# A fused linear-attention, mixture and routed-expert kernel: the mixture's last expert in plain products, routing on fifteen tiles instead of twelve

## The chip, the cores and the metric

The kernel runs on one core of a Trainium2 chip. The metric is the time in microseconds (us) of one execution on the device, as the median of several; lower is better. PE (TensorE) does the matmuls, and PEld is its weight load; DVE (VectorE), ACT (ScalarE) and POOL (GpSimd) do elementwise work; SP and POOL issue the DMAs spoken of here.

## The reference

Three stages over 2304 tokens of width 512 (8 heads of 64):

```
kv  = einsum('bhsd,bhde->..', k, v);  out = q @ kv;  x = out / rms(out) * g_norm      # per head
p   = domain_probs / (domain_probs.sum(-1) + 1e-9)                                    # 4 experts, all of them for every token
x   = sum over e of p[:, e] * (relu(x @ w1[e]) @ w2[e])                                # w1[e] 512x1024, w2[e] 1024x512
...
idx = argmax(normalised x @ normalised expert_emb.T / tau)                             # 8 experts, one for each token
out[idx == e] = gate_w * (relu(x[idx == e] @ w1b[e]) @ w2b[e])
```

The second mixture's router needs a token's finished sum over all four experts of the first one.

## The kernel before, in words

**Precision.** Each product is done as three matmuls of operands split in a high and a low part (hi*hi, hi*lo, lo*hi): ACT casts the high part (L61), DVE subtracts it to get the low part (L62 for weights, L768 `hl` for hidden values).

**Attention** of a tile of 128 tokens is a chain: transpose of q (`qt_unit`, `psq` L142), product with kv (`x_unit`, `psx` L159, copied by ACT to `xs` L173), RMS-norm on DVE (`x_norm`, from L175), transpose back (`xt_unit`, `psxt` L204). `att(tiles)` lists these for one or two tiles. They are scattered over the phases of the first mixture.

**First mixture.** The 18 tiles form 6 units of 3 tiles, and the units 3 pairs p = 0, 1, 2. A phase (p, e, fh) does one pair, one expert e, one half fh of its 1024 hidden columns: first L1 (x times w1, L793), then L2 (hidden times w2, L888), whose result DVE scales and adds to the tile's sum, `acc` (L897); the last such sum of tiles 12 to 17 goes to `fin`. From the second expert on, L1 is done by Strassen's scheme (7 products for 8) on sums of blocks of x (`x_fills`: b11, t1 and so on, made on POOL and DVE) and of w1 (`w1_sums`). Expert 0 of pair 0 is done in four plain phases, one unit and one half each (`plain_unit`, L781). `run_steps(steps, todo, pace)` writes a phase out: after each step come the pieces of `todo` that are due by a hand-written time (in model units; a Strassen phase is about 30 long, a plain one 16.6), and `background(n)` takes n pieces of a queue `bg` with n from `pace`: logits and routing. The order in which the code is written is the order on each engine; an engine waits in place.

**Routing.** When a tile's sum is done it is written to DRAM, `x1d`. Its router logits come in one of two ways: `logits_v` reloads it as `row` and does eight dot products on DVE (L314); `logits_t` transposes it on PE (`pslt` L324) and multiplies by the embeddings (`psl` L329). `route_a` runs once the first TA = 12 tiles have logits: it counts tokens per expert (`psr` L393), gives each its place, builds one-hot matrices `po` on DVE (L338), and inverts the placement by matmuls (`psi` L454) to indices `ix`. From these, `gather` fetches the token rows of NA = 4 full jobs (`xg` L694). `route_b` does the same for all the other tokens after tile 17.

**Second mixture.** 25 slots of 128 tokens (22 filled for this data), each: gather, transpose (`pstx` L1136), w1 (`m1`, `psm` L1146), w2 (L1168), scaled output `y` on ACT (L1172), scatter. A slot's weights, 8 DMAs of 512 KB, are loaded only where the expert changes.

Of the kernel before, what the change touches and what calls it, by code (L numbers as in the profile page):

```python
# [20 lines left out]
def attn_moe_moe_kernel(ctx: ExitStack, tc: tile.TileContext, q, k, v, g_norm, dprobs, w1, w2, emb, tau, w1b, w2b, out):  # L21
    nc = tc.nc
# [995 lines left out]
    sm = st_p.tile([128, NT, 1], F32, name="sm", tag="sm")
    nc.vector.tensor_reduce(out=sm, in_=dp, axis=AX.X, op=ALU.add)
    nc.vector.tensor_scalar_add(sm, sm, 1e-9)  # L1020
    nc.vector.reciprocal(sm, sm)
    nc.vector.tensor_tensor(out=dp, in0=dp, in1=sm.to_broadcast([128, NT, E1]), op=ALU.mult)
# [27 lines left out]
    order = [(0, 0), (0, 1), (1, 1), (1, 0)]  # L1050
    for at_ph, (un, fh) in enumerate(order):
        steps = [(P1T / 4, lambda f=f: plain_unit(un, f)) for f in range(4)]
        steps += l2_steps(0, fh, [un], None, first_half, (P2T - P1T) / 6)
        todo = []
        if at_ph != 2:
            todo += spread([lambda n=n: fill_w2(0, 2 * fh + n) for n in range(2)], 0, P1T)
        if at_ph == 0:
            w1_blocks(0, 1)
            todo += [(-1, f) for f in plain_direct(1)]
            todo += [(2.5, lambda: nc.gpsimd.tensor_tensor(  # L1060
                out=xr[:, 0].rearrange("p c n -> p (c n)"), in0=xf_t[0][:, 0:2 * XW].bitcast(F32), in1=xf_t[1][:, 0:2 * XW].bitcast(F32), op=ALU.add))]
            todo += [(1.5 + 2 * p, lambda p=p: kv_unit(1, p)) for p in range(NP)]
            todo += [(7.9, lambda: w1_blocks(0, 2)), (16.0, lambda: w1_blocks(0, 3))]
            todo += spread(plain_direct(2), 8.5, 12) + spread(plain_direct(3), 16.1, 16.6)
            todo += spread(att(range(TS, TS + 1)), 9, P2T)
        if at_ph == 1:
            todo += spread(att(range(TS + 1, 2 * TS)), 0, 13)
            todo += [(13.2, lambda: x_split(6, xblock(0, 1))), (14.5, xs_f["b22"])]
        if at_ph == 2:
            todo += [(7.9, lambda: w1_blocks(0, 0)), (12.0, lambda: w1_blocks(0, 1))]  # L1070
            todo += spread(plain_direct(0), 8.5, 12) + spread(plain_direct(1), 12.1, 16)
            todo += spread([xs_f[n] for n in ("t1", "t3", "x1", "x3", "t2", "x2", "t4")], 0, P2T)
        if at_ph == 3:
            todo += [(7.5, lambda: w1_sums(1, 0)), (8.5, xs_f["x4"])]
            todo += spread(w1_fills(1, 0), 9, 12) + [(12.1, lambda: w1_sums(1, 1))] + spread(w1_fills(1, 1), 12.2, P2T)
        run_steps(steps, todo, [0] * len(steps))

    ahead = {
        (0, 1, 0): spread(att([6]), 16, S2T),
# [10 lines left out]
        (1, 3, 0): spread(att([17]), 0, S2T),  # L1090
        (2, 0, 0): [(20.0, end_attention)],
    }
    for at_ph, ph in enumerate(strassen):
# [13 lines left out]
        last = at_ph + 1 == len(strassen)  # L1107
        if last:
            todo += [(6.5, lambda: late.update(slots=True)), (14.7, lambda: late.update(weights=True))]
        pace = [4 if last else 0 if i % 2 else 1 for i in range(len(steps))]  # L1110
        if last:
            pace[-1] = 0
        run_steps(steps, todo, pace)
# [157 lines left out]
```

## Time and profile before

| | us |
|---|---|
| median of 3 runs (lowest, highest) | 1193.28 (1192.33, 1194.89) |
| the profiled execution | 1194.21 |
| its span, first to last instruction | 1192.4 |
| first mixture, first plain phase to last L2 matmul | 26.6 to 872.1 |
| output y of slot 1, 2 and the last used slot | 932.4, 944.7, 1174.7 |

The span is 1.8 us less than the execution's own time, and that 0.9 more than the median. Times inside the span are from its first instruction. In the timeline, a bracket at the end of a row gives the idle time of the engine before it and what it waited for.

### The profile page before, as it was taken

Reading aid. Unit: us, or ns where it says so; the run is one execution under the profiler, and the core shown is the slowest. Engines: PE = TensorE matmul, PEld = TensorE weight load, DVE = VectorE, ACT = ScalarE, POOL = GpSimd, SP = SyncE. Lnnn points to the kernel's source line nnn. Section 1 sums busy time; section 2 is a strip of 40 time slices with the busy share of each in tenths; the row PEclk is TensorE's granted clock in tenths of the full one; section 3 lists DMA queues with packets and bytes.
Section 4 is the critical chain, followed back from the end, with each engine's and each line's share of the span. In section 5 each row is a group of like instructions: output and inputs, shape, how many; then the busy total and the mean of one; then the engine's idle time right before and its main releaser. Section 6 shows DMA issues by size and latency. Waiting matters only on the chain. (4 is left out here: it accounts for less than half of the span.)

```text
span 1192.4 us, 17373 instructions
## 1 busy us (share of the span) xinstructions
PE 1116.8 (94%) x5902; PEld 974.9 (82%) x5902; DVE 754.9 (63%) x1300; ACT 566.4 (47%) x1010; POOL 292.1 (24%) x344
## 2 busy tenths in 40 slices
PE   8999999998999999999999999999784999999993
PEld 7789888997888989889889888789563888888882
DVE  3557564664986787666978878775358662465350
ACT  3435446543555444444554444344354664566450
POOL 3102333220433233212433333122010211121120
PEclk9999999999999999999999999999897999999997
DMA  9413254221334223211332222123433863665460
GB/s 257 140 48 108 79 159 133 80 71 54 106 106 133 89 72 88 71 55 52 105 108 80 75 70 77 53 71 89 139 121 138 288 216 103 210 233 212 148 218 12
DMA packets 87971, 139.18 MB, mean 117 GB/s; under 512 B 17269, under 2 KB 51061, under 8 KB 87744
## 3 DMA queue, kind: packets, MB, share of 16 engines
q1 hardware_dynamic: 80432, 113.56, 29.9%
q0 software_dynamic: 7440, 24.41, 6.1%
q8 instruction: 49, 0.80, 0.3%
q14 instruction: 50, 0.41, 0.1%
HBM read 183.03 MB, written 10.49 MB: 162 GB/s over the span
## 5 line engine op out<-in xcount | busy, mean ns | idle before, releaser
L888 PE MATMUL bank<-w2h,hh 128*128 128x512 f32 x576 | 230.8, 401 | 6.1 <-DVE acc L897 4.6
L888 PE MATMUL bank<-w2h,hl 128*128 128x512 f32 x576 | 228.0, 396 | 1.9 <-DVE hl L768 1.9
L888 PE MATMUL bank<-w2l,hh 128*128 128x512 f32 x576 | 227.3, 395 | 0.0
L62 DVE TENSOR_TENSOR w2l<-raw,w2h 128x1024 fp32r<-128x1024 f32 x98 | 117.8, 1222 | 108.5 <-ACT w2h L61 107.8
L793 PE MATMUL bank<-xth,w1h 128*128 128x384 f32 x616 | 160.8, 342 | 6.3 <-DVE acc L897 3.8
L793 PE MATMUL bank<-xtl,w1h 128*128 128x384 f32 x616 | 157.4, 336 | 0.0
L793 PE MATMUL bank<-xth,w1l 128*128 128x384 f32 x616 | 157.2, 336 | 0.0
L888 PEld LDWEIGHTS bank<-w2h,hh 128*128 128x128 f32 x576 | 109.5, 190 | 29.7 <-DVE acc L897 4.8
L888 PEld LDWEIGHTS bank<-w2h,hl 128*128 128x128 f32 x576 | 109.4, 190 | 28.7 <-DVE hl L768 5.1
L888 PEld LDWEIGHTS bank<-w2l,hh 128*128 128x128 f32 x576 | 109.6, 190 | 21.2
L897 DVE SCALAR_TENSOR_TENSOR acc<-bank,dp,acc 128x512 f32<-128x512 f32 x120 | 89.6, 746 | 52.9 <-PE bank L888 52.5
L793 PEld LDWEIGHTS bank<-xth,w1h 128*128 128x128 f32 x616 | 109.8, 189 | 11.4 <-ACT w1h L61 4.6
L793 PEld LDWEIGHTS bank<-xtl,w1h 128*128 128x128 f32 x616 | 112.0, 189 | 0.0
L793 PEld LDWEIGHTS bank<-xth,w1l 128*128 128x128 f32 x616 | 111.7, 188 | 0.0
L61 ACT CAST w2h<-raw 128x1024 fp32r<-128x1024 f32 x98 | 101.3, 1056 | 3.7 <-DMA raw<-in_moe_w_dram 2.5
L62 DVE TENSOR_TENSOR w1l<-raw,w1h 128x512 fp32r<-128x512 f32 (+2 forms) x131 | 87.7, 690 | 24.2 <-ACT w1h L61 23.2
L804 POOL TENSOR_TENSOR sv<-sv,s 128x384 f32<-128x384 f32 x44 | 47.5, 1079 | 225.9 <-ACT sv L800 215.9
L800 ACT COPY s<-bank 128x384 f32<-128x384 f32 x88 | 42.1, 478 | 102.9 <-PE bank L793 102.9
L606 POOL TENSOR_TENSOR wsum<-raw 128x256 f32<-128x256 f32 x44 | 37.9, 862 | 189.7 <-issue 141.2
L61 ACT CAST w1h<-wsum 128x1024 fp32r<-128x1024 f32 x44 | 46.1, 1048 | 72.4 <-POOL wsum L609 72.4
L314 DVE CUSTOM_DVE_ANT_0 scr<-row,en_b 128x512 bf16<-128x512 f32 x96 | 78.0, 813 | 0.1
L1173 POOL DMA_INDIRECT out_dram<-y,ix x22 | 22.4, 1019 | 217.3 <-ACTq L734 95.1
(246 smaller groups left out, 1973.3 us busy)
## 6 DMA issues: line engine op xcount, KB each, us to landing
raw<-in_moe_w_dram SPq DMA_DIRECT2D x300, 512.0 KB
raw<-in_k_dram SPq DMA_DIRECT2D x12, 256.0 KB
raw<-in_v_dram SPq DMA_DIRECT2D x12, 256.0 KB
qraw<-in_q_dram POOLq DMA_DIRECT2D x12, 256.0 KB, 4.0
x1d<-acc POOLq DMA_DIRECT2D x12, 256.0 KB, 2.5
row<-x1d POOLq DMA_DIRECT2D x12, 256.0 KB, 4.3
en_b<-in_moe_expert_emb_dram POOLq DMA_DIRECT2D x1, 2048.0 KB
x1d<-fin POOLq DMA_DIRECT2D x6, 256.0 KB, 2.3
```

What stands on the lines that cost most here:

```text
L61: nc.scalar.copy(hi, raw)
L62: (eng or nc.vector).tensor_tensor(out=lo, in0=raw, in1=hi.bitcast(F32), op=ALU.subtract)
L314: nc.vector.tensor_tensor_reduce(out=scr, in0=x, in1=en_b[:, e], scale=1.0, scalar=0.0, op0=ALU.mult, op1=ALU.add, accum_out=lg[:, t, e:e + 1]
L606: gt(out=sm[:, 0], in0=a21, in1=a22, op=ALU.add)
L793: nc.tensor.matmul(out=ps, lhsT=wform(wo, b, w)[:, c], rhs=xform(xo, x)[:, c], start=start and n == 0, stop=(n == 5), skip_group_check=True)
L800: nc.scalar.copy(t, src)
L804: (eng or nc.vector).tensor_tensor(out=out, in0=a, in1=b, op=ALU.add)
L888: nc.tensor.matmul(out=ps, lhsT=h_t[o][f][u][:, ns], rhs=w[j][:, a], start=(k == 0 and m == 0), stop=(k == 3 and m == 2))
L897: nc.vector.scalar_tensor_tensor(out=fin, in0=ps, scalar=dp[:, t, e:e + 1], in1=ac, op0=ALU.mult, op1=ALU.add)
L1173: nc.gpsimd.indirect_dma_start(out=out[:, :], out_offset=bass.IndirectOffsetOnAxis(ap=ix[:, col(s):col(s) + 1], axis=0), in_=y, in_offset= ...
```

## The change

- NA, NB become 8 and 17, TA 15 tiles: `route_a` takes tiles 0 to 14 and makes 8 full jobs.
- The last expert of the last pair is done in four plain phases: unit 4 with halves 0 and 1, then unit 5 with halves 1 and 0. Tiles 12 to 14 are so finished two phases before the first mixture's end. The first of w1's and w2's halves is loaded a second time (2 MB more). One block of x that the Strassen scheme has overwritten is rebuilt in the last Strassen phase (`x_back`: three sums and a split on DVE).
- `logits_v` is used for tiles 0 to 13, `logits_t` from 14 on.
- In `att` of two tiles, the first tile's `xt_unit` comes ahead of the second's `x_unit`.
- In the first phase, the normalising of the mixture's weights `dp` moves from ahead of the phase into it, and a sum `xr`, one 128x1536 addition on POOL, becomes four 128x384 on DVE.
- Of the block sums between pairs, two (t3, x3) come earlier and three (b21, t4, x4) go into the next pair's first phase.

```
-    NA, NB, R = 4, 21, 5
-    TA = 4 * TS
+    NA, NB, R = 8, 17, 5
+    TA = 5 * TS
...
+        return [
+            step(xform(0, 2).bitcast(F32), xform(1, 2), ALU.add),
+            step(t, xform(0, 5), ALU.subtract),
+            step(t, xform(1, 5), ALU.subtract),
+            lambda: x_split(6, t),
+        ]
...
+    stream += raws(E1 - 1, 0) + raws(E1 - 1, 1) + raws(E1 - 1, 0)
...
-        last = e == E1 - 1 and fh == 1
+        last = e == E1 - 1 and fh == ((t // TS) % 2 == 0 or t < N // 128 - 2 * TS)
...
-            bg.append((logits_v if t < TA else logits_t)(t, ac))
+            bg.append((logits_v if t < TA - 1 else logits_t)(t, ac))
...
             u.append(lambda t=t: qt_unit(t))
+            if prev is not None:
+                u.append(lambda t=prev: xt_unit(t))
             u.append(lambda t=t: x_unit(t))
             u.append(lambda t=t: x_norm(t))
-            if prev is not None:
-                u.append(lambda t=prev: xt_unit(t))
             prev = t
...
+    def plain_phase(un, e, fh, todo, pace):
+        steps = [(P1T / 4, lambda f=f: plain_unit(un % 2, f)) for f in range(4)]
+        steps += l2_steps(e, fh, [un], None, first_half, (P2T - P1T) / 6)
+        run_steps(steps, todo, pace)
...
-            todo += [(2.5, lambda: nc.gpsimd.tensor_tensor(
...
+    todo += [(1.5 + 2 * p, lambda p=p: kv_unit(1, p)) for p in range(NP)] + [(6.0, norm_probs)]
+    todo += [(10.0 + c, lambda c=c: nc.vector.tensor_tensor(
+        out=xr[:, 0, c], in0=xform(0, 0, 2)[:, c].bitcast(F32), in1=xform(1, 0, 2)[:, c].bitcast(F32), op=ALU.add)) for c in range(NC)]
...
+            todo += [(14.8 + 2 * i, f) for i, f in enumerate(x_back())]
...
-            todo += [(4.0, xs_f["b11"]), (4.2, xs_f["t1"])]
-            todo += spread([xs_f[n] for n in ("x1", "t2", "x2", "b22", "t3", "x3", "b21", "t4", "x4")], 14.8, 26)
...
+            todo += [(4.0, xs_f["b11"]), (5.5, xs_f["t1"]), (7.0, xs_f["t3"]), (10.0, xs_f["x3"])]
+            todo += spread([xs_f[n] for n in ("x1", "t2", "x2", "b22")], 14.8, 26)
+            carried = [(0.5, xs_f["b21"]), (3.0, xs_f["t4"]), (6.0, xs_f["x4"])]
...
+    e, u = E1 - 1, UNITS - 2
+    plain_phase(u, e, 0, w2_fills(e, 0) + w1_plain_fills(e, 1), [1] * 99)
+    plain_phase(u, e, 1, w2_fills(e, 1), [1] * 99)
+    plain_phase(u + 1, e, 1, w1_plain_fills(e, 0), [2] * 99)
+    todo = w2_fills(e, 0) + [(7.5, lambda: late.update(slots=True)), (8.3, lambda: late.update(weights=True))]
+    plain_phase(u + 1, e, 0, todo, [4] * 9 + [0])
```

Code behind the diff's first new lines stands 12 to 29 lines further down than before: L897 is L914 in the changed kernel, L888 L905, L768 L785, L1136 L1165.

Three places in the order of the instructions. First DVE, in the first phase, between the last split of the first tiles and the second half of w1's splits (`sm`, `dp`: the mixture's weights; `w1l`, `w2l`, `hl`: low parts). Before:

```order
L212 SCALAR_TENSOR_TENSOR xtl<-psxt,g_74,xth 128x4x128 x3
L1019 TENSOR_REDUCE sm<-dp 128x18
L1020 TENSOR_SCALAR sm<-sm 128x18
L1021 RECIPROCAL sm<-sm 128x18
L1022 TENSOR_TENSOR dp<-dp,sm 128x72
L768 SCALAR_TENSOR_TENSOR hl_133<-bank,hh_125 128x384
L62 TENSOR_TENSOR w1l<-raw,w1h 128x512
L62 TENSOR_TENSOR w1l<-raw,w1h 128x256 x2
L62 TENSOR_TENSOR w2l_87<-raw,w2h_85 128x1024
```

After:

```order
L785 SCALAR_TENSOR_TENSOR hl_133<-bank,hh_125 128x384
L62 TENSOR_TENSOR w1l<-raw,w1h 128x512
L62 TENSOR_TENSOR w1l<-raw,w1h 128x256 x2
L62 TENSOR_TENSOR w2l_87<-raw,w2h_85 128x1024
L785 SCALAR_TENSOR_TENSOR hl_135<-bank,hh_127 128x384
L785 SCALAR_TENSOR_TENSOR hl_137<-bank,hh_129 128x384
L1037 TENSOR_REDUCE sm<-dp 128x18
L1038 TENSOR_SCALAR sm<-sm 128x18
L1039 RECIPROCAL sm<-sm 128x18
L1040 TENSOR_TENSOR dp<-dp,sm 128x72
```

The four instructions on `sm` and `dp` now stand behind the first low parts of w1 and w2. Second PE, in L2 of phase (0,3,0), where tiles 10 and 11 get their attention. Before:

```order
L142 MATMUL psq<-ident,qraw 128x128 x4
...
L888 MATMUL bank<-w2h_85,hl_135 128x512
L159 MATMUL psx<-kvbd_142,qT 128x128 x4
...
L888 MATMUL bank<-w2h_86,hl_138 128x512
L204 MATMUL psxt<-ident,xs 128x128 x4
```

After:

```order
L142 MATMUL psq<-ident,qraw 128x128 x4
...
L905 MATMUL bank<-w2h_85,hl_135 128x512
L204 MATMUL psxt<-ident,xs 128x128 x4
...
L905 MATMUL bank<-w2h_85,hl_133 128x512
...
L159 MATMUL psx<-kvbd_142,qT 128x128 x4
```

The transpose of tile 10 (`psxt`), which reads the only buffer `xs`, stands ahead of tile 11's product instead of 5 groups of L2 behind it. Third DVE, at the first mixture's end (`fin`: the sum of tile 17; `gs`, `ix`: the inverted placement). After:

```order
L334 TENSOR_TENSOR rhs<-so,ids 128x15x8 x2
L334 TENSOR_TENSOR rhs<-so,gp 128x15x8 x3
L914 SCALAR_TENSOR_TENSOR fin<-bank,dp,acc_124 128x512
L338 TENSOR_SCALAR po<-lane_b,pos 128x128 x15
L461 COPY gs<-psi 128x8
L462 SCALAR_TENSOR_TENSOR ix<-gs,psi 128x8
L463 COPY gs<-psi 128x8
L334 TENSOR_TENSOR gs<-gs,psi 128x8 x2
L62 TENSOR_TENSOR xtl<-raw,xth 128x1024 x4
L334 TENSOR_TENSOR xgl<-pstx,xgh 128x512
```

On PE the 15 `psi` of `route_a` stand behind the last L2 matmul, right ahead of slot 0's `pstx`. Before, `route_a`'s `po` came in phase (2,3,0), with its 12 `psi` among that phase's L1 matmuls, and what stood behind the last L2 matmul was slot 0 itself; `route_b`'s 18 `po` stood behind the first slot.

## Rows read from the trace of the kernel before

**Rows 1.** The page: busy time, share of the span, instructions of the engines.
```profile
PE 1116.8 (94%) x5902; PEld 974.9 (82%) x5902; DVE 754.9 (63%) x1300; ACT 566.4 (47%) x1010; POOL 292.1 (24%) x344
```

**Rows 2.** Stretches: length, busy PE, PEld, DVE, ACT, POOL (instructions), PEclk, DMA share, GB/s.
```profile
26.60:43.14 16.54, 14.17 (x129) 12.12 (x129) 10.36 (x14) 6.33 (x15) 4.92 (x4) 0.90 0.61 155
53.22:78.33 25.11, 22.92 (x127) 20.10 (x126) 13.21 (x27) 11.88 (x21) 1.78 (x2) 0.93 0.30 85
78.33:94.86 16.53, 16.53 (x86) 15.08 (x85) 10.11 (x15) 7.45 (x14) 0.00 (x0) 1.00 0.08 27
247.59:288.70 41.11, 36.52 (x189) 32.66 (x188) 23.15 (x40) 16.92 (x32) 10.30 (x13) 0.96 0.22 65
321.82:339.41 17.59, 17.59 (x96) 17.55 (x97) 15.86 (x29) 9.45 (x18) 9.47 (x11) 0.90 0.55 165
624.62:655.57 30.95, 30.95 (x158) 28.10 (x156) 25.64 (x48) 14.28 (x27) 10.09 (x11) 1.00 0.25 77
751.45:786.95 35.50, 32.54 (x162) 28.31 (x160) 27.92 (x70) 14.40 (x27) 7.70 (x10) 1.00 0.19 60
940.00:953.00 13.00, 13.00 (x67) 10.90 (x66) 12.03 (x14) 11.72 (x16) 2.55 (x2) 1.00 0.99 351
```

**Rows 3.** What PE's matmuls waited for, 100 to 787 us: total, times, longest.
```profile
PE bank L793 <- DVE acc L897: 3.8, 2, 1.9
```

**Rows 4.** Timeline of PE, places with idle time: start, length, idle before.
```profile
36.23 0.69 PE L781 MATMUL bank<-xth,w1l 128*128 128x384 f32 x1 [2.37 <-DVE w1l L62]
...
72.14 0.41 PE L204 MATMUL psxt<-ident,xs 128*128 128x128 f32 x2 [2.19 <-DVE xs L181]
...
281.05 0.50 PE L888 MATMUL bank<-w2h,hh 128*128 128x512 f32 x1 [4.59 <-DVE acc L897]
...
873.53 0.48 PE L1146 MATMUL psm<-xth,xgh 128*128 128x512 f32 x1
...
920.36 3.04 PE L454 MATMUL psi<-rhs,po 128*128 128x105 bf16 x18 [15.45 <-DVE po L338]
```

**Rows 5.** Timeline of DVE and POOL in the first phase.
```profile
31.30 3.81 DVE L1022 TENSOR_TENSOR dp<-dp,sm 128x72 f32<-128x72 f32 x1
...
31.53 3.48 POOL L1060 TENSOR_TENSOR xr<-xth,xtl 128x1536 f32<-128x1536 f32 x1
...
35.50 1.34 DVE L62 TENSOR_TENSOR w1l<-raw,w1h 128x512 fp32r<-128x512 f32 x3
```

**Rows 6.** Timeline of DVE in the second half of phase (0,3,0).
```profile
277.12 0.69 DVE L175 TENSOR_REDUCE ms<-xs 128x8 f32<-128x512 f32 x1 [8.24 <-ACT xs L173]
```

**Rows 7.** The tile row: its instructions on DVE; its reloads.
```profile
L314 DVE CUSTOM_DVE_ANT_0 scr<-row,en_b x96: 669/684/1522, 320.3 to 739.4; 128x512 bf16<-128x512 f32 x96
...
DMA to landing us min/median/max: 3.0/3.4/5.7
```

**Rows 8.** Groups by line and form on DVE, 787 to 932 us.
```profile
L62 DVE TENSOR_TENSOR w2l<-raw,w2h 128x1024 fp32r<-128x1024 f32 x12 | 14.4, 1218 | 9.7 <-ACT w2h L61 9.7
L897 DVE SCALAR_TENSOR_TENSOR fin<-bank,dp,acc 128x512 f32<-128x512 f32 x6 | 4.5, 749 | 8.1 <-PE bank L888 8.1
L768 DVE SCALAR_TENSOR_TENSOR hl<-bank,hh 128x384 fp32r<-128x384 f32 x4 | 2.2, 554 | 1.3 <-ACT hh L765 1.3
```

**Rows 9.** Timeline of DVE at the end of the second routing.
```profile
911.75 0.23 DVE L338 TENSOR_SCALAR job<-job,ho 128x21 f32<-128x21 f32 x1
...
917.06 0.18 DVE L334 TENSOR_TENSOR gp<-ga,gp 128x18 bf16<-128x18 f32 x1
...
920.06 3.01 DVE L338 TENSOR_SCALAR po<-lane_b,pos 128x128 bf16<-128x128 bf16 x18
```

**Rows 10.** The gathers of token rows: issue to landing.
```profile
DMA to landing us min/median/max: 3.3/4.2/7.9
```

**Rows 11.** Timeline of ACT: the outputs y of slots 1 and 2.
```profile
932.41 0.70 ACT L1172 ACTIVATE y<-psy,gs 128x512 f32<-128x512 f32 x1
...
944.68 0.70 ACT L1172 ACTIVATE y<-psy,gs 128x512 f32<-128x512 f32 x1
```

More of the change, by code (lines that the diff above doesn't have):

```diff
@@ L648, in x_fills, with x_back, step @@
         }
+    def x_back():
+        t = sum_p.tile([128, 4, 2, 128], F32, name="wsum", tag="wsum").rearrange("p a b c -> p (a b c)")[:, 0:XW]
+        t = t.rearrange("p (c t) -> p c t", t=SUB)
+        def step(a, b, op):
+            return lambda: nc.vector.tensor_tensor(out=t, in0=a, in1=b.bitcast(F32), op=op)
+        return [
[4 more added lines that the diff above has]
+        ]
     def raws(e, fh):
@@ L653, in attn_moe_moe_kernel @@
     stream += [("kv", 0, n) for n in range(NP)] + raws(0, 0) + raws(0, 1) + raws(0, 0)
-    strassen = [(p, e, fh) for p in range(UNITS // 2) for e in range(E1) for fh in range(2) if p or e]
+    END = (UNITS // 2 - 1, E1 - 1)
+    strassen = [(p, e, fh) for p in range(UNITS // 2) for e in range(E1) for fh in range(2) if (p or e) and (p, e) != END]
     KV_AT = {(0, 2, 0): 2, (1, 0, 1): 3}
@@ L895, in l2_unit @@
         else:
-            fin = late["tmp"].tile([128, D], F32, name="fin", tag="fin", bufs=2) if last and t >= TA else ac
+            fin = late["tmp"].tile([128, D], F32, name="fin", tag="fin", bufs=3) if last and t >= TA else ac
             nc.vector.scalar_tensor_tensor(out=fin, in0=ps, scalar=dp[:, t, e:e + 1], in1=ac, op0=ALU.mult, op1=ALU.add)
@@ L1017, in attn_moe_moe_kernel, with norm_probs @@
     issue()
[L1018 to L1022, printed above, removed]
+    def norm_probs():
+        sm = st_p.tile([128, NT, 1], F32, name="sm", tag="sm")
+        nc.vector.tensor_reduce(out=sm, in_=dp, axis=AX.X, op=ALU.add)
+        nc.vector.tensor_scalar_add(sm, sm, 1e-9)
+        nc.vector.reciprocal(sm, sm)
+        nc.vector.tensor_tensor(out=dp, in0=dp, in1=sm.to_broadcast([128, NT, E1]), op=ALU.mult)
     setup_route()
@@ L1047, in first_half @@
         return 0 if t % (2 * TS) < TS or t >= 2 * TS else 1
-    xs_f = x_fills()
[L1050 to L1059, printed above, removed]
-            todo += [(2.5, lambda: nc.gpsimd.tensor_tensor(
[L1061 to L1076, printed above, removed]
@@ new lines, in plain_phase, with w2_fills, w1_plain_fills @@
+    def plain_phase(un, e, fh, todo, pace):
+        steps = [(P1T / 4, lambda f=f: plain_unit(un % 2, f)) for f in range(4)]
+        steps += l2_steps(e, fh, [un], None, first_half, (P2T - P1T) / 6)
+        run_steps(steps, todo, pace)
+    def w2_fills(e, fh, t0=0, t1=P1T):
+        return spread([lambda n=n: fill_w2(e, 2 * fh + n) for n in range(2)], t0, t1)
+    def w1_plain_fills(e, fh):
+        n = 2 * fh
+        return (
+            [(7.9, lambda: w1_blocks(e, n)), (12.0, lambda: w1_blocks(e, n + 1))]
+            + spread(plain_direct(n), 8.5, 12) + spread(plain_direct(n + 1), 12.1, 16)
+        )
@@ new lines, in attn_moe_moe_kernel @@
+    xs_f = x_fills()
+    w1_blocks(0, 1)
+    todo = w2_fills(0, 0) + [(-1, f) for f in plain_direct(1)]
+    todo += [(1.5 + 2 * p, lambda p=p: kv_unit(1, p)) for p in range(NP)] + [(6.0, norm_probs)]
+    todo += [(10.0 + c, lambda c=c: nc.vector.tensor_tensor(
+        out=xr[:, 0, c], in0=xform(0, 0, 2)[:, c].bitcast(F32), in1=xform(1, 0, 2)[:, c].bitcast(F32), op=ALU.add)) for c in range(NC)]
+    plain_phase(0, 0, 0, todo + w1_plain_fills(0, 1) + spread(att([TS]), 9, P2T), [0] * 99)
+    todo = w2_fills(0, 1) + spread(att(range(TS + 1, 2 * TS)), 0, 13)
@@ L1078, in attn_moe_moe_kernel @@
+    plain_phase(0, 0, 1, todo + [(13.2, lambda: x_split(6, xblock(0, 1))), (14.5, xs_f["b22"])], [0] * 99)
+    todo = w1_plain_fills(0, 0) + spread([xs_f[n] for n in ("t1", "t3", "x1", "x3", "t2", "x2", "t4")], 0, P2T)
+    plain_phase(1, 0, 1, todo, [0] * 99)
+    todo = w2_fills(0, 0) + [(7.5, lambda: w1_sums(1, 0)), (8.5, xs_f["x4"])]
+    todo += spread(w1_fills(1, 0), 9, 12) + [(12.1, lambda: w1_sums(1, 1))] + spread(w1_fills(1, 1), 12.2, P2T)
+    plain_phase(1, 0, 0, todo, [0] * 99)
     ahead = {
@@ L1092, in attn_moe_moe_kernel @@
     }
+    carried = []
     for at_ph, ph in enumerate(strassen):
@@ L1096, in attn_moe_moe_kernel @@
         steps += l2_steps(e, fh, [2 * p, 2 * p + 1], (0, 1, 2, 0, 1, 3), lambda t: 0, (S2T - S1T) / 12)
-        todo = spread([lambda n=n: fill_w2(e, 2 * fh + n) for n in range(2)], 1, 6) + ahead.get(ph, [])
+        todo = w2_fills(e, fh, 1, 6) + ahead.get(ph, []) + carried
+        carried = []
         if at_ph + 1 < len(strassen):
@@ L1102, in attn_moe_moe_kernel @@
             todo += [(19.1, lambda n=n: w1_sums(e2, n + 1))] + spread(w1_fills(e2, n + 1), 23, 28)
+        else:
+            todo += [(10.4, lambda: w1_blocks(E1 - 1, 0)), (19.1, lambda: w1_blocks(E1 - 1, 1))]
+            todo += spread(plain_direct(0), 13, 19) + spread(plain_direct(1), 23, 28)
+            todo += [(14.8 + 2 * i, f) for i, f in enumerate(x_back())]
         if e == E1 - 1 and fh == 1 and p + 1 < UNITS // 2:
             xs_f = x_fills()
-            todo += [(4.0, xs_f["b11"]), (4.2, xs_f["t1"])]
-            todo += spread([xs_f[n] for n in ("x1", "t2", "x2", "b22", "t3", "x3", "b21", "t4", "x4")], 14.8, 26)
[L1107 to L1113, printed above, removed]
+            todo += [(4.0, xs_f["b11"]), (5.5, xs_f["t1"]), (7.0, xs_f["t3"]), (10.0, xs_f["x3"])]
+            todo += spread([xs_f[n] for n in ("x1", "t2", "x2", "b22")], 14.8, 26)
+            carried = [(0.5, xs_f["b21"]), (3.0, xs_f["t4"]), (6.0, xs_f["x4"])]
+        run_steps(steps, todo, [i % 2 for i in range(len(steps))])
+    e, u = E1 - 1, UNITS - 2
[4 more added lines that the diff above has]
+    plain_phase(u + 1, e, 0, todo, [4] * 9 + [0])
     while stake[0] < 4:
```

## The prediction

> **What bounds the kernel now.** I read the page first: PE is busy 94% of the span [rows 1], so a gain can come only from PE's idle time, from stretches in which its clock is low, or from fewer matmuls. The change takes no matmuls away (it adds some: plain products where Strassen's stood). So I looked for PE's idle and slow places with the windows of its phases, then with its waits and timeline, and for each asked what DVE, ACT or POOL did at that time.
>
> The reader is to see three kinds of stretch. First, undisturbed ones: a plain phase takes 16.53 us and a Strassen phase 30.95, PE busy throughout at a granted clock of 1.00, which is the level of 2.4 GHz; in the second mixture a slot takes 944.68 - 932.41 = 12.27 with PE at 100% [rows 2, 11]. Second, phases with a hole: the first plain phase has 2.37 us idle and a mean clock of 0.90, the second takes 25.1 us with 2.19 idle before `psxt`, (0,3,0) takes 41.1 with one hole of 4.59, the phases at 321.82 and 592.46 each begin after 1.9 idle, and (2,2,1) takes 35.5 instead of 30.95 [rows 2 to 4]. Third, the passage into the second mixture, 787 to 932 us, where PE stands 15.45 us in one piece at `psi`, waiting for `po` on DVE [rows 4].
>
> A hole costs more than itself. After the idle times the clock falls to the level of 1.2 GHz for a while: a mean of 0.90 over 16.54 us says that 0.20 of it (3.3 us) ran at half speed, 1.65 us lost; the same working gives 1.76 for the second phase, 1.64 for (0,3,0) and 1.76 for the phase at 321.82 [rows 2]. I call this the clock's share of a hole.
>
> **The change part by part.** All against the profiled execution's own 1194.2.
>
> *First phase.* PE waited 2.37 us for the split of w1 that stands, on DVE, behind the normalising of `dp`. That normalising is slow: its product took 3.81 us for 72 columns, while POOL ran the one 128x1536 addition, 3.48 us, in the same microseconds [rows 4, 5]. The change moves the first behind the splits and the second, in four pieces, onto DVE at 10 to 13 of the phase. The hole and its clock's share are 2.37 + 1.65 = 4.0. Against it DVE gets four additions, at most about 0.55 each by the `hl` of the same 384 columns [rows 8], so 2.2 us in the L2 half, where DVE is not full: it was busy 10.36 of 16.54 [rows 2]. I take 2.9 (between 0, if the added work stops PE there, and 4.0).
>
> *Second phase.* 2.19 + 1.76 = 3.95 at the `psxt` of tile 5. With two tiles in `att`, the first one's transpose now stands ahead of the second one's product. The last tile's transpose still ends the phase's chain, so I expect about half of the hole, 1.2, to stay, and its clock's share to go: 2.4 to 2.8; I take 2.4 (0 to 3.95).
>
> *(0,3,0).* ACT's copy of tile 11's `psx` into the only `xs` had to wait for tile 10's `psxt`, which stood five groups of L2 later; DVE's first norm instruction idled 8.24 us for it [rows 6], with the sums (`acc`) of finished tiles queued behind it, and PE ran out of banks for 4.59 [rows 4]. The new order takes the cause away. 4.59 + 1.64 = 6.2 (3 if tile 11's chain, now two groups later, stops the phase's last sums; 6.2 else). I take 6.2.
>
> *Ends of pairs 0 and 1.* L1 of the next phase waited 1.9 for `acc` at both, 3.8 in all [rows 3], because all sums of x-blocks stood on DVE in the last phase; the clock's share at the first is 1.76. Three of nine pieces go into the next phase, where POOL and DVE were busy 9.47 and 15.86 of 17.59 us in the L1 half alone [rows 2]: not much room. 5.5 at best; I take 4.0 (0 to 5.5).
>
> *(2,2,1).* It held `route_a` for 12 tiles: 70 DVE instructions against 48 in an undisturbed phase, 4.55 us longer [rows 2]. That goes; `x_back`'s three sums and a split come, about four instructions of 1 us on a DVE that was busy 25.64 of 30.95 [rows 2]. I take 4.2 (1 to 4.55).
>
> *The passage.* Before, from the end of (2,2,1), 786.95, to slot 1's `y`, 932.41 [rows 2, 11]: 145.5. After, step by step. Two plain phases undisturbed, 2 x 16.53 = 33.1. Then two phases in which DVE is late. In the third, tiles 12 and 13 get 16 dot products at 0.68, 10.9 [rows 7], beside three sums at 0.75, four `hl` at 0.55 and two blocks of w1 splits at 1.34 [rows 5, 8]: 18.0. In the fourth, four `hl`, two w2 splits at 1.22, three sums: 6.9 [rows 8]; some 52 small routing instructions at 0.23 (24 of them took from 911.75 to 917.24): 11.9; fifteen `po` at 3.01/18: 2.5 [rows 9]. That makes 21.3, together 39.3 on an engine that also waits for PE and ACT. DVE was busy 79% when it routed in (2,2,1) and 90% at the phase at 321.82 [rows 2]; at 85% this takes 46.2. It starts about 1.5 after the third phase begins (tile 12 is summed before that, and its reload lands 3.4 later [rows 7]): the last `po` at 47.7 of these two phases, the fourth phase itself being over at about 38 (18.0/0.85 = 21.2 for the third, then 16.5). PE idles between. `ix` 0.7 later, the gather's landing 4.2 [rows 10], its transpose and split 1.3 (estimate from the 0.55 and 0.75 above): m1 of slot 0 at 53.9. From there to `y` of slot 1 it was 932.41 - 873.53 = 58.9; without the 15.45 for the second `po` and the 3.04 of its `psi`, which no longer lie there [rows 4], 40.4, and 1.6 for the clock after the idle stretch: 42.0. In all 33.1 + 53.9 + 42.0 = 129.0, a gain of 16.5. The 18 `psi` of `route_b` come later, in the slots, where PE is the bound: -3.0 [rows 4]. Net 13.5; bounds 3 (below) and 23 (if the `po` were ready when the fourth phase ends).
>
> How the second routing hides: eight early slots, 8 x 12.27 = 98 us, lie ahead of `route_b`'s first gather, against four before, so its 18 `po` and indices have room.
>
> *More loads.* 2 MB more in phases whose DMA share is 0.2 to 0.3 [rows 2]: nothing. But the experts of this data make slots 7 to 11 load weights five times in a row, 4.19 MB each. The one stretch with such loads moved 351 GB/s at a DMA share of 0.99 with PE never idle [rows 2]: 11.95 us a slot against 12.27. Gathers and scatters come on top. I take -1.5 (0 to -16).
>
> Sum: 2.9 + 2.4 + 6.2 + 4.0 + 4.2 + 13.5 - 1.5 = 31.7, so 1162.5; the median of before lies 0.9 below the profiled execution, so **1161.6**.
>
> **The rivals.**
>
> *The routing is later than that.* DVE at 79% instead of 85% is 3.5 more; a gather at its longest, 7.9, is 3.7 more [rows 10]; `fin` of tile 17, which DVE does ahead of `po`, or the last tiles' logits waiting behind w1 splits, 3 more. Then the passage gives 3 and the time is 1172. For it: PE's `psr` of the fourth phase stands in place after only six L2 matmuls, so that PE stops the phase with DVE. Against: the sum of work on DVE is counted in full.
>
> *The routing is covered.* If DVE's waits fall together with PE's and `po` are there by the end of the fourth phase, 9.7 more are gained: 1152.
>
> *The early holes move instead of going.* The first four edits give 5 of 15.5: 1172. For it: DVE at 15.86 of 17.59 where pieces are carried to [rows 2].
>
> *The gather is held up.* Behind the new `ix`, DVE runs four 128x1024 splits, 4 x 1.22 = 4.9 [rows 8], at once, while POOL issues the gather that slot 0 waits for. In the trace gathers landed after 4.2 us by the median, 7.9 at the longest [rows 10], which tells that some were held, not by what. If it is held for all four: 1166.5. The Trainium skill says of this, under "SBUF — State Buffer", section "SBUF: two separate sides", that DVE and GpSimd share one pair of ports as an exclusive lock, and that a DMA issued from GpSimd's queue can be starved of its descriptors while DVE holds the pair; by it the whole 4.9 would be paid, if a split with two inputs in SBUF counts as holding it, and no run here shows that yet.
>
> *Slower: the five loads in a row become the bound.* Nothing is lost at 351 GB/s. To lose 34 us, enough to be slower than before by 0.2%, five loads (20.97 MB) would have to take 5 x 12.27 + 9 (six loads of 512 KB ahead, at 351 GB/s) + 34 = 104 us: below 201 GB/s. Loads at 242 GB/s would cost 16 and give 1176. Against it: the 351 were seen over 13 us, with PE at 100% [rows 2].
>
> **How the numbers follow.** Chances: the forecast 0.56 (its own range 1156 to 1168), the later routing 0.16, moved holes 0.09, covered routing 0.09, held gather 0.06, slow loads 0.04. The range 1150 to 1174 reaches to both the 1172s and to 1152, and leaves out the slow loads and the far ends of the others, less than 0.2. Faster by over 0.2%, about what a measurement of this kernel tells from no change: 0.94; within it 0.02; slower 0.04, nearly all of it the slow loads.
>
> **What the profile after should show.** First plain phase about 16.54 - 2.9 with `w1l` not waited for; L2 of (0,3,0) without a hole and DVE's first norm instruction not idle for 8 us; the two starts of pairs without 1.9 of idle; (2,2,1) at about 31. In the passage: third plain phase some 18 long, PE idle about 10 us before `psi`, `po` last on DVE; `y` of slot 1 some 129 after the end of (2,2,1); slots 7 to 11 still 12.3 apart. The prediction is wrong if the fourth phase ends with `po` done, if slot 0 waits much longer than 5 us after `ix`, or if slots 7 to 11 are spaced by more than 13.

## The result, and the profile after

| | us |
|---|---|
| before, median of 4 runs | 1192.93 (1192.33 to 1194.89) |
| after, median of 4 runs | 1162.63 (1161.05 to 1164.03) |
| ratio, with its 95% interval | 0.9743 (0.9724 to 0.9762) |
| span of the profiled execution, before and after | 1192.4 and 1159.9 |

The change makes the kernel 2.6% faster; forecast were 1161.6 in a range of 1150 to 1174. PE's row on the page (beside [rows 1]):

```profile
PE 1109.9 (96%) x5905; PEld 971.9 (84%) x5905; DVE 762.9 (66%) x1340; ACT 560.6 (48%) x1000; POOL 276.6 (24%) x325
```

PE does about the same number of matmuls in 7 us less and idles 26 us less. The stretches of after, with the columns of [rows 2]: L1 of the first phase, the second phase, (0,3,0), L1 of (0,3,1) and of (1,0,0), (2,2,1), the third plain phase of the passage, the fourth with the wait behind it, the stretch of the routing on DVE, and one slot's period among the five loads in a row:

```profile
26.82:39.43 12.61, 12.61 (x128) 11.08 (x128) 6.91 (x14) 6.34 (x15) 1.45 (x3) 1.00 0.81 203
51.19:73.88 22.69, 21.28 (x127) 18.94 (x126) 12.12 (x25) 10.43 (x17) 1.79 (x2) 1.00 0.35 94
244.34:279.00 34.66, 34.66 (x189) 31.49 (x188) 23.21 (x40) 16.96 (x32) 10.38 (x13) 1.00 0.26 77
279.00:295.78 16.78, 15.13 (x85) 14.48 (x84) 11.69 (x13) 9.03 (x17) 6.58 (x6) 1.00 0.17 63
312.57:329.10 16.53, 16.41 (x97) 15.86 (x96) 16.35 (x29) 10.00 (x19) 8.26 (x9) 1.00 0.59 170
740.59:771.53 30.94, 30.94 (x157) 28.10 (x156) 18.88 (x30) 12.46 (x25) 2.03 (x2) 1.00 0.18 53
804.63:821.17 16.54, 16.54 (x85) 15.10 (x84) 12.62 (x32) 5.56 (x14) 1.09 (x2) 1.00 0.21 62
821.17:845.92 24.75, 19.07 (x102) 16.57 (x100) 22.14 (x80) 9.47 (x15) 1.08 (x2) 0.95 0.28 104
806.41:848.13 41.72, 36.04 (x189) 31.34 (x187) 36.97 (x124) 16.29 (x30) 2.72 (x5) 0.94 0.23 83
960.54:972.81 12.27, 12.27 (x62) 10.22 (x61) 11.29 (x13) 10.89 (x16) 2.55 (x2) 1.00 1.03 392
```

The reader is to see that (0,3,0) and (2,2,1) have lost their holes (PE busy for the whole length, clock 1.00), that the first phase's L1 is 12.61 long where it was 16.54, that PE idles 1.65 us in L1 of (0,3,1), which before was 14.71 long, and that PE stands idle 5.7 us at the first mixture's end while DVE is busy 22.14 of 24.75. The timeline of DVE and PE there (beside [rows 4, 9]):

```profile
806.41 0.69 DVE L314 CUSTOM_DVE_ANT_0 scr<-row,en_b 128x512 bf16<-128x512 f32 x1 [3.55 <-DMA row<-x1d]
...
845.61 2.52 DVE L338 TENSOR_SCALAR po<-lane_b,pos 128x128 bf16<-128x128 bf16 x15
...
845.92 2.49 PE L454 MATMUL psi<-rhs,po 128*128 128x40 bf16 x15 [5.17 <-DVE po L338]
...
852.55 1.12 PE L1165 MATMUL pstx<-ident,xg 128*128 128x128 f32 x4 [4.14 <-DMA xg<-x1d,ix]
...
854.34 0.80 PE L1175 MATMUL psm<-xth,xgh 128*128 128x512 f32 x1
```

The hole of 15.45 has become one of 5.17 and one of 4.14. The outputs `y` of slot 1, of slots 3 and 4, and of the last used slot (beside [rows 11]):

```profile
897.48 0.70 ACT L1201 ACTIVATE y<-psy,gs 128x512 f32<-128x512 f32 x1
...
921.97 0.70 ACT L1201 ACTIVATE y<-psy,gs 128x512 f32<-128x512 f32 x1
936.41 0.71 ACT L1201 ACTIVATE y<-psy,gs 128x512 f32<-128x512 f32 x1
...
1141.80 0.69 ACT L1201 ACTIVATE y<-psy,gs 128x512 f32<-128x512 f32 x1 [5.95 <-PEq L1268]
```

Slot 4 takes 14.44, 2.2 more than a period: there lie `route_b`'s 18 `psi`.

Where the 32.5 us of span come from, from the starts of the phases on PE in both traces:

| stretch | forecast | measured |
|---|---|---|
| first phase | 2.9 | 2.25 |
| second phase | 2.4 | 2.42 |
| (0,2,0) | 0 | -1.20 |
| (0,3,0) | 6.2 | 6.45 |
| last and first phases at the two ends of pairs | 4.0 | -0.89 |
| (1,0,1) to (1,3,0), (2,0,1) to (2,2,0) | 0 | 2.05 |
| (2,2,1) | 4.2 | 4.56 |
| passage, end of (2,2,1) to `y` of slot 1 | 16.5 | 19.51 |
| behind it (`route_b`'s `psi`, loads in a row) | -4.5 | -2.43 |
| start, ahead of the first phase | 0 | -0.22 |

### The profile page after: what moved, and what is told of

It reads as the page before. It is cut to its first block, busy times and chain, and to the rows that moved or that the text cites. A ratio compares the mean times of both kernels' runs of the same rounds, so it can differ in the third digit from the quotient of the medians.

```text
span 1159.9 us, 17410 instructions
## 1 busy us (share of the span) xinstructions
PE 1109.9 (96%) x5905; PEld 971.9 (84%) x5905; DVE 762.9 (66%) x1340; ACT 560.6 (48%) x1000; POOL 276.6 (24%) x325
## 5 line engine op out<-in xcount | busy, mean ns | idle before, releaser
L905 PE MATMUL bank<-w2h,hh 128*128 128x512 f32 x576 | 227.4, 395 | 1.4 <-ACT hh L782 1.4
L905 PE MATMUL bank<-w2h,hl 128*128 128x512 f32 x576 | 225.5, 391 | 0.0
L905 PE MATMUL bank<-w2l,hh 128*128 128x512 f32 x576 | 225.0, 391 | 0.0
L810 PE MATMUL bank<-xth,w1h 128*128 128x384 f32 x560 | 145.9, 341 | 5.4 <-ACT s L817 2.6
L810 PE MATMUL bank<-xtl,w1h 128*128 128x384 f32 x560 | 142.5, 335 | 0.0
L810 PE MATMUL bank<-xth,w1l 128*128 128x384 f32 x560 | 142.5, 335 | 0.0
L914 DVE SCALAR_TENSOR_TENSOR acc<-bank,dp,acc 128x512 f32<-128x512 f32 x123 | 92.0, 748 | 60.7 <-PE bank L905 60.5
L905 PEld LDWEIGHTS bank<-w2h,hl 128*128 128x128 f32 x576 | 108.2, 188 | 24.8 <-DVE hl L785 1.8
L905 PEld LDWEIGHTS bank<-w2h,hh 128*128 128x128 f32 x576 | 108.2, 188 | 24.5 <-ACT hh L782 3.8
L905 PEld LDWEIGHTS bank<-w2l,hh 128*128 128x128 f32 x576 | 108.2, 188 | 21.0
L810 PEld LDWEIGHTS bank<-xth,w1h 128*128 128x128 f32 x560 | 99.3, 188 | 10.8 <-ACT s L817 3.8
L810 PEld LDWEIGHTS bank<-xtl,w1h 128*128 128x128 f32 x560 | 101.3, 188 | 0.0
L810 PEld LDWEIGHTS bank<-xth,w1l 128*128 128x128 f32 x560 | 101.2, 188 | 0.0
L314 DVE CUSTOM_DVE_ANT_0 scr<-row,en_b 128x512 bf16<-128x512 f32 x112 | 85.8, 766 | 10.7 <-DMA row<-x1d 10.2
L817 ACT COPY s<-bank 128x384 f32<-128x384 f32 x80 | 38.5, 481 | 83.6 <-PE bank L810 83.5
L61 ACT CAST w1h<-raw 128x512 fp32r<-128x512 f32 (+2 forms) x140 | 74.1, 573 | 0.5 <-DMA raw<-in_moe_w_dram 0.3
L61 ACT CAST w1h<-wsum 128x1024 fp32r<-128x1024 f32 x40 | 42.1, 1052 | 63.3 <-POOL wsum L609 63.3
```

Source lines behind the costliest of these rows:

```text
L61: nc.scalar.copy(hi, raw)
L314: nc.vector.tensor_tensor_reduce(out=scr, in0=x, in1=en_b[:, e], scale=1.0, scalar=0.0, op0=ALU.mult, op1=ALU.add, accum_out=lg[:, t, e:e + 1]
L810: nc.tensor.matmul(out=ps, lhsT=wform(wo, b, w)[:, c], rhs=xform(xo, x)[:, c], start=start and n == 0, stop=(n == 5), skip_group_check=True)
L817: nc.scalar.copy(t, src)
```

## The experiments

Each was run beside the kernel before on the same chip, so the ratios compare best; the changed kernel's is 0.9743 (0.9724 to 0.9762). In the profiled executions of all the experiments but the first, not in that of the changed kernel, PE waits 0.4 to 2.7 us for `hn` on ACT in one of the last, conditional slots. Effects of 1 to 3 us are therefore read from the stretch that was edited.

**Eight early slots in the kernel before, and the forced place in the changed one.** Two edits that take the passage's gain apart:

```
-    NA, NB, R = 4, 21, 5
+    NA, NB, R = 8, 17, 5
```

> The kernel before with NA, NB = 8, 17 and nothing else (with 12 tiles and this data eight full jobs exist). Theory A, the hole of 15.45 us at psi came from the place where the second routing is forced (slot 2 with four early jobs), and eight early slots alone remove it: the hole goes, the 18 psi come later, y of slot 1 some 127 us after the end of (2,2,1) instead of 145.5, time 1193 - 17 = 1176 (1172 to 1180). Theory B, the last expert in plain products and the 15 tiles are what brings the passage's gain: less than 5 us, 1188 or more.

```
-        while min(s + 2, NS - 1) >= known[0] or (s + 2 >= NA and "placed" not in late):
+        while min(s + 2, NS - 1) >= known[0] or (s >= 2 and "placed" not in late):
```

> The changed kernel, with all of the second routing forced at slot 2 as in the kernel before, instead of slot 6. Theory A: PE waits at psi for po after slot 2's w1 product, 10 to 16 us, and 1 to 2 for the clock behind it, less nothing: 1173 to 1180. Theory B: tiles 12 to 14 being out of the way, the chain of the last three tiles is done by then: no hole over 3 us, 1161 to 1166.

The first: 1178.87, ratio 0.9883 (0.9853 to 0.9912). (2,2,1) ends at 785.27 in it, and `y` of slot 1 comes 126.9 later, where it was 145.5 before and is 125.95 after the whole change. Its window of (2,2,1), and the row of that `y` in ACT's timeline:

```profile
749.73:785.27 35.54, 32.55 (x162) 28.30 (x161) 28.15 (x70) 14.43 (x27) 7.71 (x10) 1.00 0.20 60
```

```profile
912.16 0.70 ACT L1172 ACTIVATE y<-psy,gs 128x512 f32<-128x512 f32 x1
```

The second: 1178.57, ratio 0.989 (0.9857 to 0.9924), with the hole back in PE's timeline:

```profile
903.02 3.02 PE L454 MATMUL psi<-rhs,po 128*128 128x85 bf16 x18 [13.81 <-DVE po L338]
```

Theory A holds both ways: eight early slots alone shorten the passage by 18.6 us, where the whole change shortens it by 19.5, and forcing the routing early costs 13.8 and about 2 more. Behind `y` of slot 1 the first kernel needs 5.45 us more than before, the changed one 2.4, and (2,2,1) keeps its 35.5. So plain products and fifteen tiles bring 0.9 + 3.0 + 4.6 = 8.5 us, outside the wait that they look made for. (That first kernel serves this data alone, in which twelve tiles have eight full jobs. For all data twelve tiles guarantee five: 1536 tokens, of which at most 8 x 127 lie in jobs not full. Fifteen guarantee eight, so the early slots need the fifteen tiles.)

**Attention in the order of before**, in the changed kernel (`xt_unit` of the first tile back behind `x_norm` of the second):

> The changed kernel with the attention of two tiles in the order of before. My account: (0,3,0) is 41.1 instead of 34.7 long with a hole of about 4.6, and the second phase's last part is up to 1 us longer: +6.4 to +7.5, 1169 to 1170. Rival, other edits have removed the hole as well: within 2 us of 1162.6.

1171.64, ratio 0.9835 (0.9803 to 0.9867). (0,3,0) is 41.75 long, 7.1 more, and the second phase 0.8 more; the span is 10.1 longer, and the wait for `hn`, 2.3 here, is about the rest. The rows of before are back, to within a hundredth ([rows 4, 6]), in DVE's and in PE's timeline:

```profile
274.75 0.69 DVE L175 TENSOR_REDUCE ms<-xs 128x8 f32<-128x512 f32 x1 [8.24 <-ACT xs L173]
```

```profile
278.68 0.79 PE L905 MATMUL bank<-w2h,hh 128*128 128x512 f32 x1 [4.60 <-DVE acc L914]
```

After the change that DVE instruction waits 0.76. Of the second phase's 2.42 only 0.8 are the attention's order. The other 1.6 belong to no edit: the kernel with eight early slots has the second phase of before, with the same hole of 2.19 at `psxt`, and took 23.50 for it where the profiled execution before took 25.11 [rows 2]; this run, with the hole back too, took 23.49. The granted clock of the phase is 1.00 in both, and was 0.93 before. The windows of that phase, with eight early slots and in this run:

```profile
53.12:76.62 23.50, 21.31 (x127) 18.96 (x126) 13.21 (x27) 11.91 (x21) 1.78 (x2) 1.00 0.27 91
```

```profile
51.27:74.76 23.49, 21.30 (x128) 18.94 (x126) 12.14 (x25) 10.36 (x17) 1.78 (x2) 1.00 0.31 91
```

**Block sums of x at the times of before**, and then the carried ones alone:

```
-            todo += [(4.0, xs_f["b11"]), (5.5, xs_f["t1"]), (7.0, xs_f["t3"]), (10.0, xs_f["x3"])]
-            todo += spread([xs_f[n] for n in ("x1", "t2", "x2", "b22")], 14.8, 26)
-            carried = [(0.5, xs_f["b21"]), (3.0, xs_f["t4"]), (6.0, xs_f["x4"])]
+            todo += [(4.0, xs_f["b11"]), (4.2, xs_f["t1"])]
+            todo += spread([xs_f[n] for n in ("x1", "t2", "x2", "b22", "t3", "x3", "b21", "t4", "x4")], 14.8, 26)
```

> The changed kernel with the sums of x-blocks between pairs at the times of before. As forecast: 4 us slower (1166.6), since L1 of the next pair waits 1.9 twice. By the two traces, in which the four phases around both ends take 0.9 us more after the change than before: the holes only moved into L1 of the last phases of the pairs, 0 to 1.5 us faster (1161 to 1163).

1163.53, ratio 0.9758 (0.9725 to 0.979). The four phases at the two ends take 132.67 against 134.08 in the changed kernel: this edit, of which I had expected 4 us, costs 1.4. The view of PE's waits around the first end, 276 to 314 us, in the changed kernel:

```profile
PE bank L810 <- ACT s L817: 1.1, 1, 1.1
PE bank L810 <- DVE s L821: 0.5, 1, 0.5
```

and with the sums of before:

```profile
PE bank L810 <- DVE acc L914: 1.9, 1, 1.9
```

The hole moved from the next pair's start into L1 of the pair's last phase. In the changed kernel's trace t1 and t3 stand on DVE ahead of the sum that PE waits 0.5 for (1.78 and 1.49 long), and x3's cast on ACT (0.82) ahead of the copy that it waits 1.1 for. If they are the cause, the carried sums should be kept and the early ones not:

> The changed kernel with the block sums t1, t3 and x3 of the pairs' last phases at the times of before; only b21, t4 and x4 still go into the next pair's first phase. If the earlier t1, t3, x3 make the new holes in L1 of the pairs' last phases (ACT s, DVE s, 1.6 us each time) and the carried ones remove the 1.9 us at the next phase's start: both go, the four phases take 3 to 4 us less than in the changed kernel, 1158.5 to 1160. If the carried sums make next phases' L1 late: no better than with all fills as before, 1161 to 1163.5.

1160.41, ratio 0.9745 (0.9724 to 0.9765), between the two accounts. The stretches bear the first out: the four phases take 130.33, 3.75 less than in the changed kernel, with L1 of (0,3,1) undisturbed and only 0.7 idle in L1 of (1,0,0). The windows of these two:

```profile
279.02:293.72 14.70, 14.70 (x85) 14.54 (x84) 9.88 (x13) 8.36 (x17) 5.23 (x6) 1.00 0.22 72
310.08:327.18 17.10, 16.44 (x98) 15.85 (x97) 16.92 (x30) 9.89 (x19) 8.28 (x9) 1.00 0.57 170
```

The third plain phase starts 4.48 earlier than in the changed kernel; the whole time, with its scatter of 2 to 4 us a run, can't tell this.

**The first phase's two moves, one at a time:**

```
+    norm_probs()
     setup_route()
...
-    todo += [(1.5 + 2 * p, lambda p=p: kv_unit(1, p)) for p in range(NP)] + [(6.0, norm_probs)]
+    todo += [(1.5 + 2 * p, lambda p=p: kv_unit(1, p)) for p in range(NP)]
```

> The changed kernel with dp normalised ahead of the first phase as before; xr stays four additions on DVE. If the hole of 2.37 us came from the order on DVE (my step): the hole at w1l is back, product of dp 3.8 us, first phase 2.3 longer, 1165. If it came from POOL's long addition holding up a DVE instruction that ran beside it: the product takes about 0.23 us, the four instructions about 1 in all, the hole is under 1 us, and the first phase at most 0.5 longer, 1162 to 1163.5.

1163.51, ratio 0.9742 (0.9726 to 0.9759); the first phase is 24.38 long, as in the changed kernel, and its L1 has no hole. DVE's timeline:

```profile
31.40 0.23 DVE L1040 TENSOR_TENSOR dp<-dp,sm 128x72 f32<-128x72 f32 x1
...
32.01 1.35 DVE L62 TENSOR_TENSOR w1l<-raw,w1h 128x512 fp32r<-128x512 f32 x3
```

```
-    todo += [(10.0 + c, lambda c=c: nc.vector.tensor_tensor(
-        out=xr[:, 0, c], in0=xform(0, 0, 2)[:, c].bitcast(F32), in1=xform(1, 0, 2)[:, c].bitcast(F32), op=ALU.add)) for c in range(NC)]
+    todo += [(2.5, lambda: nc.gpsimd.tensor_tensor(
+        out=xr[:, 0].rearrange("p c n -> p (c n)"), in0=xf_t[0][:, 0:2 * XW].bitcast(F32), in1=xf_t[1][:, 0:2 * XW].bitcast(F32), op=ALU.add))]
```

> The changed kernel with xr as one addition on POOL at 2.5 of the first phase; dp stays at 6.0. By the order on DVE: w1l is not late, phase as in the changed kernel, 1161 to 1163. By POOL's addition holding up DVE: whichever DVE instruction with two inputs from SBUF meets it (w1l, w2l) takes up to 3.5 us instead of 0.4 to 1.2, PE waits 2 to 3 us in L1, 1164.5 to 1166.

1163.73, ratio 0.9731 (0.9713 to 0.975); the first phase is 23.89 long, 0.5 shorter, again with no hole in L1. POOL's and DVE's timeline:

```profile
31.26 3.52 POOL L1087 TENSOR_TENSOR xr<-xth,xtl 128x1536 f32<-128x1536 f32 x1
```

```profile
30.74 4.65 DVE L62 TENSOR_TENSOR w1l<-raw,w1h 128x512 fp32r<-128x512 f32 x3
```

The product of `dp` takes 0.23 without POOL's addition and took 3.81 beside it [rows 5]; the three splits of w1 take 1.35 without it and 4.65 beside it, of which one split alone takes 3.7. In both cases a DVE instruction with two SBUF inputs was held up for about the length of POOL's addition. But the hole needs both: the hold-up and the queue place of `dp`. With either move the splits end early enough (33.36 and 35.39; before it was 36.84), so my second expectation was wrong: the hold-up came, its price didn't. The Trainium skill states under "SBUF — State Buffer", section "SBUF: two separate sides", that the port pair of DVE and GpSimd is locked for a whole instruction; in length these rows agree. Which of the two came first they do not settle: the product of `dp` began 0.23 ahead of POOL's addition [rows 5], the long split 0.09 behind it.

**Less work on DVE ahead of `po`.** The condition that chooses the way of the logits, with TA - 3 (tiles 12, 13) and TA - 2 (tile 13, with the block sums of before):

```
-            bg.append((logits_v if t < TA - 1 else logits_t)(t, ac))
+            bg.append((logits_v if t < TA - 3 else logits_t)(t, ac))
```

> The changed kernel with the logits of tiles 12 and 13 by transposes on PE instead of 16 dot products on DVE. If the 5.2 us of PE before psi are DVE's work alone, as I have it: 12.2 us less on DVE, po ready before the fourth phase ends, hole at psi gone, gather earlier by 5 to 7, against 2 x 1.5 us of PE for transposes: 1158.5 to 1161. If something else holds the routing (round trips to PE and ACT): hole still over 3, 1162 to 1165.

> The changed kernel with tile 13's logits too on PE (tile 12's stay on DVE) and the fills of before. With both tiles on PE, PE paid some 5.6 us in the second and third plain phase for the 5.2 at psi. If half of the move balances the two engines: hole at psi 0 to 1, plain phases 2 longer, against the changed kernel 3 less from this and 1.6 less from the fills: 1157.5 to 1160.5. If each tile on PE costs as much as it gives: only the fills' part, 1160.5 to 1163.

Both miss. With two tiles 1166.64, ratio 0.9763 (0.9741 to 0.9785): the hole at `psi` is gone, but the second plain phase takes 20.29 instead of 16.55 and the third 18.42, and the gather's wait grows to 7.07. With one tile 1163.60, ratio 0.9764 (0.9743 to 0.9785): the third phase takes 19.56, and PE stops in the fourth instead of behind it (PE's timeline):

```profile
836.51 0.80 PE L905 MATMUL bank<-w2h,hh 128*128 128x512 f32 x1 [4.09 <-ACT hh L782]
```

PE gives back what DVE gains, or more: from the third phase's start to `y` of slot 1 the profiled execution with one tile, the slowest of the five, takes 97.7, where the changed kernel takes 92.85. Why ACT was late at that `hh` was not followed further.

**The gather's gap.** PE waits 4.14 for slot 0's rows; the logits of tiles 15 to 17, which stand behind slot 0's transpose, were put ahead of it, all three or (with the block sums of before) one:

```
-    tx_unit(0)
-    background(4)
+    for _ in range(4):
+        background(4)
+    tx_unit(0)
```

> The changed kernel with the logits of tiles 15 to 17 issued on PE ahead of slot 0's transpose, in the 4.1 us in which PE waits for the gather, instead of between slot 0's and 1's products. If that wait is the gather's own latency: PE fills it, the waits of 0.6 and 2.4 us at psl fall into it, m1 of slot 0 starts 0 to 2 later, y of slot 1 comes 2 to 5 earlier: 1157.5 to 1161. If the last tile's logits are late anyway (DVE busy with the four splits): slot 0 starts 4 to 5 later, 1162 to 1165.

> The changed kernel with the logits of tile 15 alone, instead of three tiles, ahead of slot 0's transpose in the gather's 4.1 us, and the fills of before. Three tiles took 11 us there at the low clock. One should take 3.6, which the gap covers: slot 0 starts no later, m1 of slot 0 loses one insertion of 1.1 to 1.5: 1159.5 to 1161.5. If the low clock lasts longer for it or the gather's transpose queues behind it: 1162 or more.

Three: 1168.20, ratio 0.9775 (0.9757 to 0.9794), beyond both accounts; from the third phase's start to `y` of slot 1 it is 2.0 slower than the changed kernel. The three tiles take from 848.29 to 859.49, a chain of PE, ACT and DVE with PE's granted clock at 0.50, the level of 1.2 GHz, behind the hole of 5.16 at `psi` (PE's timeline, the first of them and the start of the second):

```profile
848.29 1.10 PE L324 MATMUL pslt<-ident,fin 128*128 128x128 f32 x4
850.12 1.88 PE L329 MATMUL psl<-en_t,xx 128*128 128x8 f32 x8 [0.73 <-ACT xx L325]
851.85 1.09 PE L324 MATMUL pslt<-ident,fin 128*128 128x128 f32 x4
```

One (a loop of 2, which also puts the next tile's transposes there): 1159.78, ratio 0.9736 (0.9715 to 0.9757). One tile takes 3.6 us and fits; PE's wait for the gather is 0.4 (PE's timeline):

```profile
850.87 1.12 PE L1164 MATMUL pstx<-ident,xg 128*128 128x128 f32 x4 [0.39 <-DMA xg<-x1d,ix]
```

From the third phase's start `y` of slot 1 comes 90.6 later, against 92.85 in the changed kernel. Without the tile in the gap but with the same block sums it came 91.8 later, so that the edit is worth 1.2 to 2.3.

**Three together** (carried sums alone, tile 13 on PE, tile 15 in the gap):

> The changed kernel with the three edits together (only b21, t4, x4 carried; tile 13's logits on PE; tile 15's logits in the gather's gap). If they add up, each by its favourable account: 1155 to 1158.5. If they take the same idle time of PE: 1159 to 1162.

1156.48, ratio 0.9699 (0.9677 to 0.9721), the fastest kernel here, in the range of the favourable account, though the tile on PE brought nothing by itself. The first and the third edit's 3.75 and 1.2 to 2.3 us are about what the ratios differ by, 0.0044 or 5.2 us. The two intervals lie side by side (up to 0.9721, from 0.9724), so this gain is near the limit of what the runs can tell. The sum without the tile on PE was not tried; from the third phase's start to `y` of slot 1 it takes 91.0 here and took 90.6 with the tile in the gap alone, so nothing shows that the tile on PE helps. (In the profiled execution, the slowest of the five, PE's clock was at 0.82 through the first 15 us of the first phase, which took 26.82 where the changed kernel takes 24.37; no edit touches that phase.)

## Why the prediction was right, by its steps

**(0,3,0)** (6.2, measured 6.45): right in cause and size; the order of attention alone brings the hole and the 8.24 us back.

**(2,2,1)** (4.2, measured 4.56): right; `x_back` is hidden on a DVE that is busy 18.88 of 30.94.

**The passage** (16.5, measured 19.51): right in mechanism, 3 us short in size. The term that was mis-sized is the routing on DVE: I had 39.3 us of work at 85% busy, 46.2; it was 36.97 at 89%, 41.72. And its backlog did not stop PE in the third phase (16.54 where I had 21.2). PE stood 5.17 before `psi`, not the 10 of my list of signs, since `po` came earlier and the `psi` began before the last of them. So m1 of slot 0 began 49.7 after the third phase's start, not 53.9; from there to `y` of slot 1 it took 43.1, where I had 42.0. What I had wrong in emphasis is which edit earns it: eight early slots, not the plain phases.

**`route_b`'s `psi` and the loads in a row** (-3.0 and -1.5, measured -2.43 together): the `psi` cost 2.2 in slot 4; the five loads cost nothing, at up to 392 GB/s with PE at 100%.

**First and second phase** (2.9 and 2.4, measured 2.25 and 2.42): the sums fit. The first rests on a hold-up that [rows 5] showed and I named, but I put the hole to the queue place; it takes both. I also took the 16.54 of [rows 2] for the phase and its share of DVE for the L2 half; it is L1 alone. L1 gained 3.93, about the 4.0 I had, and L2 lost 1.68, where I allowed 1.1. Its windows before and after:

```profile
43.14:53.22 10.08, 10.08 (x57) 8.46 (x53) 3.96 (x11) 4.43 (x11) 0.96 (x1) 1.00 0.45 132
```

```profile
39.43:51.19 11.76, 10.30 (x57) 8.38 (x53) 7.00 (x18) 6.09 (x14) 0.97 (x1) 1.00 0.38 113
```

PE now waits 1.46 there for `xs` on DVE. The four additions are 0.5 of the loss, by the run with the sum on POOL; the rest, which may be w1's last splits, now in this half, was not taken apart. The second phase's size is luck: the attention's order gives 0.8 of it, and 1.6 are the clock, which fell behind the hole of 2.19 in the profiled execution before and not in the two runs above that have this hole. So I had no ground to book the clock's share of every hole as a gain.

**Ends of pairs** (4.0, measured -0.89): the step that failed. I counted holes that go and allowed for the phase that the sums are carried to, not for L1 of the phase in which t3 and x3 come earlier and t1 a little later: PE waits 1.65 there at the first end. With these three at their old places and the other three still carried, the four phases take 2.86 less than before, of the 4.0. The rival of holes that move was right here, and in part in the first phase.

**Not in the sum**: (0,2,0) became 1.20 longer. `run_steps` now takes pieces of the background queue at odd steps where it took them at even ones, and the set-up of the embeddings, seven small DVE instructions, stands ahead of tile 8's norm instead of behind it; `psxt` waits 1.02. The 2.05 gained in the later phases hold the same edit's work, shifted dot products; they were not taken apart.

**The held gather**: it did not come. The gather's issue began 0.23 us ahead of the four splits, and PE took its rows up 3.46 after the issue's start, with the splits running (DVE's and POOL's timeline):

```profile
849.32 4.64 DVE L62 TENSOR_TENSOR xtl<-raw,xth 128x1024 fp32r<-128x1024 f32 x4
```

```profile
849.09 1.04 POOL L711 DMA_INDIRECT xg<-x1d,ix  x1 [2.55 <-DVE gs L463]
```

In the run with two tiles on PE the splits began first, by 0.5; issuing took 1.64, not the splits' 4.6, and PE took the rows up 5.0 after its start, 0.9 behind the splits' end. The changed kernel's 24 gathers take 0.94 to 1.54 to issue, so this one case does not tell whether the splits held it up (POOL's timeline):

```profile
849.64 1.64 POOL L711 DMA_INDIRECT xg<-x1d,ix  x1 [0.44 <-DVE gs L334]
```

## What to carry to other kernels

A wait at a place where the program forces work to be done is shortened first by moving the place: one constant, four early jobs to eight, gave nearly half of this change's gain (14.8 of 32.5 us of span). Check then what makes the constant allowed: here it is fifteen tiles instead of twelve, for all data. When work is moved earlier to clear a hole, cost the phase that it is moved into, engine by engine, and not only the one that it leaves. Work put into this idle gap of PE ran at a granted clock of 0.50 and paid its round trips to other engines: measure such work against the gap's length (one tile fitted in 4.1 us, three took 11). And compare a phase in two executions of the same code before you put its time down to an edit: the second phase differed by 1.6 us between two that share it.
